# A decode block on one core: K in 64 KB packets with a two-part softmax, wo in one load, and the last transpose through a bf16 PSUM tile

## The chip, the cores and the metric

One core of a Trainium2 chip runs the whole program. The metric is the device time of one execution in microseconds (us); the kernel before takes 420.02 us, the median of three executions (419.86 to 420.03). "Landing" is the moment when a load's completion record of a DMA engine appears in the trace; a load has 16 of them, one from each engine, and I give the first and the last where they differ. "Lead" is how long before the landing (first engine) of the load ahead of it a load is issued: a positive lead means that the queue still has work when the next load arrives.

## The reference

Two batch rows with one token each, model width 1024, 32 query heads and 4 key-value heads of width 128, a cache of 32768 rows, and an MLP of width 3584. All inputs are bf16.

```python
    mod = (_silu(c) @ w_mod).reshape(c.shape[0], 6, 1, -1)
    sa, ca, ga, sb, cb, gb = ...                                  # six rows of mod
    h = _layernorm(x) * (1 + ca) + sa
    # attention: q = h @ wq; scores = q k^T * Dh ** -0.5; p = softmax(scores); (p v) @ wo
    x = x + ga * _A_ref(h, A_k_cache, A_v_cache, A_wq, A_wo)
    h = _layernorm(x) * (1 + cb) + sb
    # MLP: y = layernorm(h); gelu(y @ w1 + b1) @ w2 + b2
    x = x + gb * _B_ref(h, B_w1, B_b1, B_w2, B_b2)
```

There are 8 pairs of batch row and key-value head. Each pair has a K and a V of 32768 x 128 bf16, which is 8.4 MB each: 64 KB on each of 128 partitions. They are the bulk of the 178 MB that the kernel reads.

## The kernel before

One queue, issued from SyncE, brings everything in a fixed order into a ring of 160 KB per partition: w_mod, wq, then K and V of 8 rounds, then wo, w1, w2. A load is issued when the readers of the memory that it overwrites are done. K uses bytes 0 to 64 KB in two halves, V uses 64 to 128 KB.

```python
    def add_k(i, hf):
        add(("K", i, hf), [2, TPC * D], A_k_cache[i % 2, i // 2].rearrange("(p h c t) d -> h p c (t d)", h=2, c=2, p=128)[hf], hf * 32 * KB, f"K{hf}")

    def add_v(i):
        add(("V", i), [NCH, TPC * D], A_v_cache[i % 2, i // 2].rearrange("(p c t) d -> p c (t d)", c=NCH, p=128), 64 * KB, "V")
    # ...
    for i in range(NBG):
        add_k(i, 0)
        add_k(i, 1)
        add_v(i)
    for m, off in enumerate((128, 0)):
        add(("wo", m), [16, DM], A_wo[m * 2048:(m + 1) * 2048, :].rearrange("(p j) n -> p j n", j=16), off * KB)
```

A round works through four chunks of 8192 cache rows. PE turns K in groups of eight 128x128 tiles into PSUM (`tr`), VectorE (DVE) or ScalarE (ACT) evacuates each group, and PE multiplies it with the query (`qk`). Only after the last chunk come one maximum, the exponentials of all chunks, and then the product with V (`pv`).

```python
EVAC_PATTERN = ("dve", "act", "dve", "act", "dve", "dve", "act", "dve")
# ...
        for cc in range(NCH):
            for g8 in range(TPC // 8):
                tr(i, cc, g8)
                pipe.append((i, cc, g8))
                # ...
                if len(pipe) > PIPE:
                    qk(*pipe.pop(0))
        while pipe:
            qk(*pipe.pop(0))
        softmax_1()
        softmax_2()
        softmax_3()
        for cc in range(NCH):
            exp(cc)
        for cc in range(NCH):
            part_sum(cc)
            pv(i, cc)
        row_sums()
        extract()
        extract_2(i)
```

The last lines of the program turn the result so that it can be stored, through an fp32 PSUM tile:

```python
    pe(lambda e: e.matmul(psM[0:16, 0:128], lhsT=res_bf.rearrange("p b k -> p (b k)"), rhs=ident[:, :], start=True, stop=True),
       reads=["res_bf", "ident"], writes=["psM"])
    dve(lambda e: e.tensor_copy(res16[:, :], psM[0:16, 0:128]), reads=["psM"], writes=["res16", "c16"])
```

## Time and profile before

| | before |
|---|---|
| time, median of 3 | 420.02 us (419.86 to 420.03) |
| span of the profiled run | 418.7 us |
| busy: PE, DVE, ACT | 291.0, 209.6, 149.4 us |
| DMA queue's share of 16 engines | 98.8% |
| read | 178.28 MB, 426 GB/s over the span |
| round of the loop, V landing to V landing | 38.68 us |

The profile's page, the table of busy time by stretch and the chain are read in the prediction. This is the time line of SyncE of the kernel before (start, duration, engine, line, operation, out<-in, count):

```profile
102.47 0.33 SPq L389 DMA_DIRECT2D V<-in_A_v_cache_dram  x1
137.97 0.33 SPq L389 DMA_DIRECT2D V<-in_A_v_cache_dram  x1
174.92 0.33 SPq L389 DMA_DIRECT2D V<-in_A_v_cache_dram  x1
```

These three V are free to start when the K ahead of them has landed, which the completion records show at 108.90, 147.59 and 186.28 us (first engine). The leads are 6.4, 9.6 and 11.4 us. The queue is never near running dry.

### The profile page before, as it was taken

The numbers are of one execution on the slowest core, as the hardware profiler recorded it, in microseconds if no ns is written. First come the engines' busy times: TensorE is split into PE (matmuls) and PEld (weight loads), VectorE is DVE, ScalarE is ACT, GpSimd is POOL, SyncE is SP. The second block draws the span as 40 slices with busy tenths as digits, with TensorE's granted clock in tenths as the row PEclk, the third lists the DMA queues.
The fourth block names the chain that finished last, engine by engine and source line by source line (L and its number), as shares of the span: only waits on it lengthen the run. The fifth ranks groups of instructions, "written<-read, shape, count | busy, mean of one in ns | idle before, by whom it ended". The sixth has DMA issues, their size and how long they took to land.

```text
span 418.7 us, 11609 instructions
## 1 busy us (share of the span) xinstructions
PE 291.0 (70%) x5183; PEld 231.3 (55%) x5183; DVE 209.6 (50%) x423; ACT 149.4 (36%) x179; POOL 6.8 (2%) x29
## 2 busy tenths in 40 slices
PE   1407449766996895699369957976995699564536
PEld 1104219762993794299149926962894399221214
DVE  1201105546677676467726664766477567620411
ACT  2000015533565364256405632643365166400100
POOL 3000000000000000000000000000000000000000
PEclk9999557986896997799589958986697889576585
DMA  9989999999999999999999999999999999899995
GB/s 373 450 380 449 448 404 493 398 406 446 441 432 429 423 451 429 419 454 457 391 435 476 407 416 448 438 438 426 438 438 426 416 460 457 377 448 428 424 427 249
DMA packets 5581, 178.42 MB, mean 426 GB/s; under 512 B 698, under 2 KB 706, under 8 KB 964
## 3 DMA queue, kind: packets, MB, share of 16 engines
q1 hardware_dynamic: 5572, 178.28, 98.8%
q8 instruction: 8, 0.13, 0.1%
q14 instruction: 1, 0.01, 0.0%
HBM read 178.28 MB, written 0.00 MB: 426 GB/s over the span
## 4 chain that ended last, share of the span: by engine, by line
DMA 71%; PE 24%; DVE 2%; issue 1%; ACT 1%; SPq 1%
DMA V<-in_A_v_cache_dram 39%; DMA wo<-in_A_wo_dram 10%; DMA K<-in_A_k_cache_dram 10%; PE psZ L584 10%; DMA w<-in_B_w_dram 9%; PE psKT L536 8%; DMA wmod<-in_w_mod_dram 4%; PE psS L548 1%; PE psZ L548 1%; PE psS L655 1%; PE psZ L729 1%; PE psZ L469 1%; ACT KT_sb L540 0%; PE psS L469 0%; DVE m1c L553 0%
## 5 line engine op out<-in xcount | busy, mean ns | idle before, releaser
L536 PE MATMUL psKT<-ident,K 128*128 128x128 bf16 x2048 | 163.1, 229 | 11.5 <-DMA K<-in_A_k_cache_dram 11.5
L540 ACT ACTIVATE KT_sb<-psKT 128x1024 bf16<-128x1024 bf16 x96 | 98.2, 1025 | 124.4 <-PE psKT L536 124.4
L542 DVE COPY KT_sb<-psKT 128x1024 bf16<-128x1024 bf16 x160 | 106.7, 688 | 61.6 <-PE psKT L536 61.2
L536 PEld LDWEIGHTS psKT<-ident,K 128*128 128x128 bf16 x2048 | 126.7, 102 | 13.0 <-DMA K<-in_A_k_cache_dram 12.7
L584 PE MATMUL psZ<-V,E_sb 128*32 128x512 bf16 x512 | 46.4, 541 | 23.2 <-DMA V<-in_A_v_cache_dram 20.0
L548 PE MATMUL psS<-qcur,KT_sb 128*128 128x8 bf16 x1024 | 44.7, 167 | 2.2 <-issue 2.2
L584 PEld LDWEIGHTS psZ<-V,E_sb 128*32 128x32 bf16 x512 | 18.7, 130 | 47.7 <-issue 38.8
L548 PE MATMUL psZ<-qcur,KT_sb 128*128 128x8 bf16 x1024 | 43.0, 167 | 2.2 <-issue 1.5
L548 PEld LDWEIGHTS psS<-qcur,KT_sb 128*128 128x128 bf16 x1024 | 40.0, 97 | 2.3 <-issue 2.3
L548 PEld LDWEIGHTS psZ<-qcur,KT_sb 128*128 128x128 bf16 x1024 | 37.9, 96 | 3.4 <-issue 1.6
L572 ACT ACTIVATE E_sb<-S_sb 128x512 bf16<-128x512 f32 x32 | 19.5, 630 | 29.6 <-DVE S_sb L570 29.6
L570 DVE TENSOR_TENSOR S_sb<-S_sb,gmb 128x512 f32<-128x512 f32 x32 | 20.0, 685 | 0.3
L576 DVE TENSOR_REDUCE rs<-E_sb 128x8 f32<-128x512 bf16 x32 | 19.7, 675 | 0.0
L469 PE MATMUL psS<-wmod,inT 128*32 128x512 bf16 x32 | 5.1, 624 | 16.2 <-DMA wmod<-in_w_mod_dram 16.2
L553 DVE TENSOR_REDUCE m1c<-psZ 128x8 f32<-128x512 f32 x16 | 11.1, 693 | 10.2 <-ACT S_sb L552 10.1
L595 DVE RECIPROCAL rinv<-psM 128x1 f32<-128x1 f32 x8 | 1.3, 168 | 27.7 <-PE psM L593 27.7
L605 PE MATMUL psM<-msum,hmat 128*128 128x128 f32 x16 | 4.2, 347 | 13.3 <-DVE msum L600 13.3
L559 PE MATMUL psM<-identf,m 128*8 128x128 f32 x16 | 4.3, 369 | 13.1 <-DVE m L556 13.1
L553 DVE TENSOR_REDUCE m1c<-psS 128x8 f32<-128x512 f32 x16 | 11.1, 693 | 3.2 <-ACT S_sb L552 3.1
L552 ACT ACTIVATE S_sb<-psZ 128x512 f32<-128x512 f32 x16 | 9.5, 595 | 7.5 <-PE psZ L548 7.5
L477 DVE COPY S_sb<-psS 128x512 f32<-128x512 f32 x1 | 0.7, 690 | 22.9 <-PE psS L469 22.9
L469 PEld LDWEIGHTS psS<-wmod,inT 128*32 128x32 bf16 x32 | 1.1, 132 | 19.3 <-DMA wmod<-in_w_mod_dram 18.0
(123 smaller groups left out, 167.5 us busy)
## 6 DMA issues: line engine op xcount, KB each, us to landing
K<-in_A_k_cache_dram SPq DMA_DIRECT2D x16, 4096.0 KB, 27.1
wq<-in_A_wq_dram SPq DMA_DIRECT2D x2, 4096.0 KB, 44.8
wo<-in_A_wo_dram SPq DMA_DIRECT2D x2, 4096.0 KB, 39.0
w<-in_B_w_dram SPq DMA_DIRECT2D x2, 3584.0 KB, 32.5
wmod<-in_w_mod_dram SPq DMA_DIRECT2D x1, 6144.0 KB, 29.8
w<-in_B_w_dram SPq DMA_DIRECT2D x3, 2048.0 KB, 37.8
wmod<-in_w_mod_dram SPq DMA_DIRECT2D x1, 4608.0 KB, 15.8
wmod<-in_w_mod_dram SPq DMA_DIRECT2D x1, 1536.0 KB, 6.0
```

What stands on the lines that cost most here:

```text
L469: pe(lambda e, w=it.view, k=k, kk=kk, ch=ch, n=n, q=q: e.matmul(bank[n][32 * q:32 * q + 32, :], lhsT=inT[:, k, :], rhs=w[:, kk, ch * 512:( ...
L536: pe(lambda e, kq=kq, jj=jj, w=kt, t=t: e.transpose(psKT[kq][:, jj * 128:(jj + 1) * 128], w[:, t, :], ident[:, :]), reads=[it.reg, "ident" ...
L540: act(lambda e, src=src: e.activation(KT_sb[g8][:, :, :], src, ACT.Copy), reads=[f"psKT{kq}"], writes=[f"KT_sb{g8}"], sem=f"ev{cc}_{g8}")
L542: dve(lambda e, src=src: e.tensor_copy(KT_sb[g8][:, :, :], src), reads=[f"psKT{kq}"], writes=[f"KT_sb{g8}"], sem=f"ev{cc}_{g8}")
L548: pe(lambda e, t=t, jj=jj: e.matmul(ps[:, t * HPG:(t + 1) * HPG], lhsT=KT_sb[g8][:, jj, :], rhs=qcur[:, :], start=True, stop=True), reads= ...
L552: act(lambda e: e.activation(Sc, ps.rearrange("p (t h) -> p h t", h=HPG), ACT.Copy), reads=[preg], writes=[f"S_sb_{cc}"], sem=f"sc{cc}")
L553: dve(lambda e: e.tensor_reduce(m1c[:, :, cc], ps.rearrange("p (t h) -> p h t", h=HPG), AX.X, ALU.max), reads=[preg], writes=[f"m1c{cc}"])
L559: pe(lambda e: e.matmul(psM[0:HPG, 0:128], lhsT=m1[:, :], rhs=identf[:, :], start=True, stop=True), reads=["m1", "identf"], writes=["psM"])
L570: dve(lambda e: e.tensor_tensor(Sc, Sc, gmb[:, :].unsqueeze(2).to_broadcast([128, HPG, TPC]), ALU.subtract), reads=[f"S_sb_{cc}", "gmb"], ...
L572: act(lambda e: e.activation(Ec, Sc.rearrange("p h (u t) -> p u h t", t=4), ACT.Exp, scale=SCALE), reads=[f"S_sb_{cc}"], writes=[f"E_sb_{c ...
L576: dve(lambda e: e.tensor_reduce(rs4[:, :, cc], Ec.rearrange("p u h t -> p h u t"), AX.XY, ALU.add), reads=[f"E_sb_{cc}"], writes=[f"rs4_{c ...
L584: pe(lambda e, t4=t4, tg=tg, q=q: e.matmul(psO[32 * q:32 * q + 32, :], lhsT=E_sb[:, tg // 4, :, :].rearrange("p h t -> p (h t)"), rhs=vt[: ...
```

## The change

The intent is to load K in one transfer with 64 KB to a partition, and wo as well, so that the same bytes go in half the packets. A whole K lands later than half a K, and it occupies one slot until all of it has been read. Two things pay for that. VectorE copies chunks 2 and 3 of K to a 32 KB side buffer, so that the slot comes free after two chunks. The softmax works in two parts, so that the product with V starts right behind the scores: chunks 0 to 2 with their own maximum, chunk 3 with its own, and weights bring the two together. The evacuation alternates evenly between VectorE and ScalarE, and the last transpose goes through a bf16 PSUM tile. The core of the diff:

```diff
+KC_AT = 128 * 1024
-W2_ITEMS = ((0, 8, 96), (8, 16, 112), (16, 24, 128), (24, 27, 144), (27, 28, 150))
-EVAC_PATTERN = ("dve", "act", "dve", "act", "dve", "dve", "act", "dve")
+W2_ITEMS = ((0, 8, 96), (8, 16, 112), (16, 24, 0), (24, 27, 16), (27, 28, 22))
+KEEP = {(0, 1): 0, (0, 3): 1, (0, 5): 2, (1, 1): 3}
 ...
-    def add_k(i, hf):
-        add(("K", i, hf), [2, TPC * D], ...[hf], hf * 32 * KB, f"K{hf}")
+    def add_k(i):
+        rows = A_k_cache[i % 2, i // 2].rearrange("(p c t) d -> p c (t d)", c=NCH, p=128)
+        if i:
+            add(("K", i), [NCH, TPC * D], rows, 0, "K", view=kv)
+            by_key["K2", i] = by_key["K", i]
+        else:
+            add(("K", i), [2, TPC * D], rows[:, 0:2, :], 0, sem="K", view=kv[:, 0:2, :])
+            add(("K2", i), [2, TPC * D], rows[:, 2:4, :], 32 * KB, sem="K2", view=kv[:, 2:4, :])
 ...
-    for m, off in enumerate((128, 0)):
-        add(("wo", m), [16, DM], ..., off * KB)
+    add(("wo", 0), [32, DM], A_wo.rearrange("(p j) n -> p j n", j=32), 0)
 ...
-        if EVAC_PATTERN[g8] == "act":
+        if g8 % 2:
 ...
+    def keep(i, n):
+        it = need("K2", i)
+        lo = n % 2 * 32 * D
+        dve(lambda e: e.tensor_copy(kc[:, n // 2, lo:lo + 32 * D], kv[:, 2 + n // 2, lo:lo + 32 * D]), reads=[it.reg], writes=[f"kc{n}"], sem=f"kc{n}")
 ...
                 tr(i, cc, g8)
+                if (cc, g8) in KEEP:
+                    keep(i, KEEP[cc, g8])
 ...
+                if (cc, g8) == (3, 2):
+                    max_1()
+                if (cc, g8) == (3, 4):
+                    max_2(0)
+                if (cc, g8) == (3, 6):
+                    max_3(0)
+        exp(0)
+        exp(1)
         while pipe:
             qk(*pipe.pop(0))
-        softmax_1()
-        softmax_2()
-        softmax_3()
-        for cc in range(NCH):
-            exp(cc)
-        for cc in range(NCH):
-            part_sum(cc)
-            pv(i, cc)
-        row_sums()
-        extract()
+        exp(2)
+        pv(i, 0)
+        max_2(1)
+        part_sum(0)
+        pv(i, 1)
+        max_3(1)
+        exp(3)
+        weights()
+        pv(i, 2)
+        part_sum(1)
+        part_sum(2)
+        weights_2()
+        extract(0)
+        pv(i, 3)
+        part_sum(3)
+        row_sums()
+        row_sums_2()
+        extract(1)
         extract_2(i)
 ...
-    pe(lambda e: e.matmul(psM[0:16, 0:128], lhsT=res_bf..., rhs=ident[:, :], start=True, stop=True), ...)
-    dve(lambda e: e.tensor_copy(res16[:, :], psM[0:16, 0:128]), ...)
+    pe(lambda e: e.transpose(psKT[0][0:16, 0:128], res_bf.rearrange("p b k -> p (b k)"), ident[:, :]), ...)
+    dve(lambda e: e.tensor_copy(res16[:, :], psKT[0][0:16, 0:128]), ...)
```

The places not shown set up the weights, the side buffer, other places in the ring for w1, the reordered extraction of the attention result into one tile `atT` for all heads, and the single loop over wo.

## The prediction

> **What bounds the kernel now.** I read the page's slices and queue table first, then the table of busy time by stretch, then the chain that ended last, then the order of time around single rounds and the tail. The page:
>
> ```profile
> PE   1407449766996895699369957976995699564536
> DMA  9989999999999999999999999999999999899995
> DMA packets 5581, 178.42 MB, mean 426 GB/s; under 512 B 698, under 2 KB 706, under 8 KB 964
> q1 hardware_dynamic: 5572, 178.28, 98.8%
> ```
>
> PE has holes in every round; the DMA row has none from the first slice to the last. So no engine's work is the bound; the bytes are. By stretch, cut at the landings of V (columns: length, then PE, PEld, DVE, ACT, POOL busy, clock, DMA share, GB/s):
>
> ```profile
> 130.00:168.70 38.70, 28.86 (x586) 24.52 (x586) 28.11 (x54) 20.35 (x26) 0.44 (x2) 0.85 1.00 434
> 284.70:323.40 38.70, 31.20 (x584) 26.96 (x584) 23.54 (x45) 17.07 (x21) 0.44 (x2) 0.81 1.00 434
> 411.00:418.70 7.70, 5.03 (x105) 4.59 (x105) 0.73 (x4) 0.00 (x0) 0.00 (x0) 0.50 0.44 179
> ```
>
> A round of the loop (one K and one V, 16.8 MB) takes 38.7 us whatever the engines do, at DMA share 1.00 and 434 GB/s. PE is busy 29 to 31 us of it. Only the last 7.7 us leave the DMA partly idle. In the chain, "V waits" are queueing: V is issued 32 us before it lands because other transfers stand ahead of it. The chain's end and one round in order of time:
>
> ```profile
> 174.92 32.74 DMA V<-in_A_v_cache_dram
> 207.66 0.14 issue
> 207.79 5.20 PE psZ L584 x49
> 213.04 33.25 DMA V<-in_A_v_cache_dram
> ...
> 413.27 1.87 PE psZ L729 x64
> 415.17 1.03 PE psZ L729 x32
> 416.22 0.19 DVE mT L732
> 416.43 0.24 DVE res_bf L733
> 416.72 0.29 PE psM L734
> 417.03 0.28 DVE c L736
> ```
>
> The end is: last w2 bytes land (the last completion records are at 415.4 us), 8 to 32 small matmuls, two vector operations, one transposing matmul, one copy, the store. I also take from the trace's packet records, each a transfer to one partition: a 32,768-byte packet takes 1213 ns, a 65,536-byte one 2418 ns. From its completion records: a V lands 19.32 us after the K half ahead of it (149.30 to 168.62), two K halves take 19.36 us (168.62 to 187.98). The same two numbers recur in every round.
>
> **What the Trainium skill says.** (1) "DMA: Bandwidth & Descriptors", section Bandwidth, "Where 436 GB/s comes from": 16 ports of 32 bytes at 850 MHz give 435.2 GB/s as the ceiling. The loop's measured 434 GB/s agrees; there is 0.3% above it. (2) "VectorE: DVE Perf Modes", section "The perf-mode tier table": a bf16 SBUF-to-SBUF copy may run at four elements a cycle, one from PSUM at two at most. The trace has only the second: 1024 bf16 from PSUM in 688 ns, which is 1024/2/0.96 = 533 ns plus 155. No run here shows the first yet. (3) "TensorE: Matmul & The Clock Gate", Part 1: an idle window of about 3.4 us halves the PE clock and a busy one restores it. The trace agrees: granted clock 0.5 to 67.65 us, though PE had started at 62.45; eight transposes took 0.87 us before and 0.47 us after.
>
> **The change part by part.**
>
> K packets. Rounds 1 to 7 load K in one transfer, 64 KB to a partition, instead of two of 32 KB. Each of 16 DMA engines had 16 packets of 1213 ns = 19.408 us a round and now has 8 of 2418 = 19.344, so 0.064 us less; the completion records say 19.36 against 19.32, so 0.04 less. Times 7 rounds: 0.28 to 0.45 us. Round 0 keeps two halves. All of this lies on the bounding resource.
>
> wo. Two halves become one load: another 0.04 to 0.06 us by the same working. It also moves the first half of the output projection later. Before, 32 matmuls ran at 372.1 and 32 at 381.73 to 385.3. Now all 64 start near 381. At the cold 3.3 to 3.5 us per 32 that is 6.8 us, at half warm about 5.5, so the residual, the two layernorms and w1 start 1.5 to 3.3 us later. In this tail gT was ready at 402.74 and the first w2 matmuls at 403.68 waited for their data anyway; the next wait for w2 is 4.2 us (to 408.41). A delay of up to 3.3 us is swallowed there. No cost.
>
> The copy ("keep") of half of K. K now fills one 64 KB slot, which would be free only after all transposes; so the kernel copies chunks 2 and 3 to a 32 KB side buffer, four copies of 128x4096 bf16 per round on DVE. Estimate, with the skill's four a cycle and the 155 ns above: 4096/4/0.96 + 155 = 1.22 us, 4.9 us a round. DVE gives up 4 evacuations of 0.688 (2.8 us), ACT gains 4 of 1.025 (4.1 us). A few small vector operations (weights, a second maximum, four more accumulations at 0.35 us) add about 3.5 us. DVE goes from about 24 us busy a round to about 30, ACT from 17 to about 21: both under 38.7.
>
> Two-part softmax. Maximum and exponentials of chunks 0 to 2 begin before the last scores, so PV starts right behind QK instead of after the gap seen here (L548 ended near 161.6, exponentials ready at 168.4). It adds one maximum pass (two fp32 matmuls of 0.4 to 0.6 us and 0.7 us of DVE). It pays for K landing whole: before, half a K was there 9.7 us earlier.
>
> The last transpose. fp32 to bf16 cast of 128 columns from PSUM, 0.28 us, becomes bf16 to bf16; at two a cycle 67 of 133 ns go: about 0.07 us less, on the path. The matmul stays 128 columns.
>
> Sum: 0.28 to 0.45 (K), 0.04 to 0.06 (wo), eight fewer completion packets of 9 ns (0.07), 0.07 (tail): 0.4 to 0.65 us less, unless a transfer has to wait for its buffer. I take 0.42: 419.6 us.
>
> **Whether a buffer stalls the DMA** (steady round, K landed at 0, V lands at 19.3, next K at 38.7). The next K needs the first 16 groups transposed and four copies done. Before, the same 16 groups freed K at 188.40 from a start at 178.65: 9.8 us. Add 2.5 us for a cold clock and 1.5 for DVE being over full at three copies in six groups: 14 us, needed at about 17.8 (19.3 less 1.5 for issue). Slack 4 us. The next V needs PV done: QK took 21.3 us (178.65 to 199.9), plus 3 to 4 as before, plus PV with the second maximum inside, 6 to 7.5: 31 to 33 us, needed at about 37. Slack 4 us or more. Round 0 is tighter: the copies wait in DVE's order for the second K half (landed 71.9 us), so QK is held from about 66 to 74; it then pays the two halts of 1.49 and 2.24 us named "issue" that this first pass shows. K free near 84.5, needed at 88; V free near 105, needed at 107.5. That the two evacuating engines have room for the moved work shows in their groups, where the idle time ahead of them is as large as the work, and ended by PE:
>
> ```profile
> L540 ACT ACTIVATE KT_sb<-psKT 128x1024 bf16<-128x1024 bf16 x96 | 98.2, 1025 | 124.4 <-PE psKT L536 124.4
> L542 DVE COPY KT_sb<-psKT 128x1024 bf16<-128x1024 bf16 x160 | 106.7, 688 | 61.6 <-PE psKT L536 61.2
> ```
>
> **Rivals.** A: the copies run at one element a cycle (4096/0.96 = 4.3 us, 17 us in the first part of a round with 4 us of other DVE work). Then K is free at 22 us or later and each of 7 rounds halts the DMA for 4 us or more: 445 to 450 us. For it: the one copy of 128x1024 that the trace has at one a cycle took 1054 ns (a broadcast source, though). Against: source and destination are contiguous bf16 in SBUF. 3%. At two a cycle (2.3 us) the slack of 4 us still holds. B: round 0 or the first rounds are late once, by 1 to 2 us, as PE starts 8 us later and cold. Then the DMA row gets one dent and the time is 420.5 to 421.5. For it: slack of only about 2 us in my sum, and instruction halts that I cannot place exactly. 17%. C: the intended gain is larger, some per cent, because the wait of PV or of QK was on the path. Against: DMA share 1.00 in every round. Even at 435.2 GB/s throughout, 178.28 MB take 409.7 us, and with some 2 us of start and the 4 us tail 415 or so: 1.2% is the most that anything can bring without fewer bytes. 1% for over 2%.
>
> **Range and chances.** The centre is 419.6; the spread of the three runs before is 0.17 us. Low end 419.1, if the full packet sum counts and the tail gives a little more; high end 420.9, with one late buffer. Faster by over 2% would need under 411.6: 0.01. Slower by over 2% needs over 428.4, rival A or a stall in each round: 0.04. Same: 0.95.
>
> **What would show each step.** Right: 65,536-byte packets for K, DMA share 1.00 and 434 GB/s in each round, rounds shorter by about 0.04 us, K issued 3 us or more before V ends, and the copies near 1.2 us each. PE's time would lie in one block per round with one wait, for K, in place of two. The last copy would be near 0.21 us. Wrong: a slice of DMA under 9 inside the loop, a K or V issue later than the landing of the transfer before it, copies over 3 us, or a w2 matmul that waits for gT after its data have landed.

## The result

| | before | after |
|---|---|---|
| time, median of 6 (range) | 420.01 us (419.86 to 420.07) | 419.76 us (419.61 to 421.40) |
| packets | 5581 | 4429 |

The six runs of the changed kernel are 421.40, 419.80, 419.61, 420.25, 419.64 and 419.73 us. The ratio of times, after over before, is 1.0002 with a 95% interval of 0.9987 to 1.0017: the same. (A ratio is the mean time of one kernel's runs over the mean of the other's of the same rounds, so it is not quite the ratio of the medians quoted.) So the median fell by 0.25 us while the mean did not fall at all, because two of the six runs are late by 0.5 and 1.7 us. The kernel before has none like the second of these: in all 46 of its runs told here the highest is 420.55 us. The profile happened to be taken in the run of 421.40 us, so the page below is of a late run. A second trace of the same kernel comes with the experiments.

The page of the changed kernel, the lines that answer to those in the prediction:

```profile
PE   1407434989499588939975995789398749956465
DMA  9989999999999999999999999999999999999994
DMA packets 4429, 178.42 MB, mean 425 GB/s; under 512 B 570, under 2 KB 578, under 8 KB 836
q1 hardware_dynamic: 4420, 178.28, 98.4%
```

There are 1152 packets fewer, the bytes are the same, and the DMA row still has no dent in the loop. What differs is the last slice, a 4 for a 5: a late end. By stretch, cut at the landings of V (length, then PE, PEld, DVE, ACT, POOL busy with counts, clock, DMA share, GB/s):

```profile
91.05:130.20 39.15, 30.79 (x544) 25.96 (x545) 28.11 (x58) 19.55 (x25) 0.51 (x2) 0.83 1.01 431
130.20:168.85 38.65, 31.05 (x621) 27.26 (x618) 28.98 (x60) 22.95 (x28) 0.51 (x2) 0.91 1.00 434
```

A round in the steady part is 38.65 us at share 1.00 and 434 GB/s. VectorE is busy 29.0 us of it, before 23.5 to 28.1 in the stretches that the prediction shows, and ScalarE 23.0 (before 17.1 to 20.4). The first stretch is 0.5 us longer than the second. The groups of the evacuation and of the new copy:

```profile
L570 DVE COPY kc<-kv 128x4096 bf16<-128x4096 bf16 x32 | 38.9, 1216 | 7.9 <-DMA kv<-in_A_k_cache_dram 7.9
L563 ACT ACTIVATE KT_sb<-psKT 128x1024 bf16<-128x1024 bf16 x128 | 128.4, 1024 | 99.5 <-PE psKT L559 99.5
L565 DVE COPY KT_sb<-psKT 128x1024 bf16<-128x1024 bf16 x128 | 88.0, 689 | 61.4 <-PE psKT L559 61.0
```

The copy takes 1216 ns; the prediction had 1.22 us from the four elements a cycle of the skill's table. Both engines still stand idle for long before their evacuations (99.5 and 61.4 us in sum), and PE ends that idle time. So neither engine became the bound.

The room is smaller than the busy times suggest, though. PE works through a round in order, waiting for DVE and ACT on the way, and where it waits for a load there is room. Two such waits of a round before (in brackets, us), and the one that is left in the changed kernel:

```profile
169.11 5.76 PE L584 MATMUL psZ<-V,E_sb 128*32 128x512 bf16 x64 [4.10 <-DMA V<-in_A_v_cache_dram]
178.65 1.96 PE L536 MATMUL psKT<-ident,K 128*128 128x128 bf16 x32 [1.31 <-DMA K<-in_A_k_cache_dram]
```

```profile
188.56 3.56 PE L559 MATMUL psKT<-ident,kv 128*128 128x128 bf16 x32 [1.27 <-DMA kv<-in_A_k_cache_dram]
```

From the third round on, PE waits for K between 0.1 and 1.6 us a round, in this trace and in the second one. From the start of a round's scores to PE's last matmul for it the chain of PE and the engines that it waits for takes 37.1 to 38.1 us of the 38.64. keep_twice below shows what happens when it takes longer.

SyncE's time line of the changed kernel shows how the leads have shrunk:

```profile
83.28 0.33 SPq L410 DMA_DIRECT2D kv<-in_A_k_cache_dram  x1
106.56 0.33 SPq L410 DMA_DIRECT2D V<-in_A_v_cache_dram  x1
125.13 0.33 SPq L410 DMA_DIRECT2D kv<-in_A_k_cache_dram  x1
143.76 0.33 SPq L410 DMA_DIRECT2D V<-in_A_v_cache_dram  x1
```

The loads ahead landed at 89.39, 108.73, 128.47 and 147.79 us (first engine), so the leads are 6.1, 2.2, 3.3 and 4.0 us. In the later rounds they lie between 4.0 and 5.6 us. The prediction counted its slack from 1.5 us before the landing. Its slack of 4 us or more in steady rounds is therefore a lead of about 5.5 us or more, and its 2.5 us (107.5 less 105) for the first V a lead of about 4. The measured leads, 4.0 to 5.6 us and 2.2 us (4.7 in the second trace), are somewhat smaller. Before, V had 6 to 12 us.

The tail of the changed kernel, from the time line:

```profile
382.51 5.59 PE L723 MATMUL psS<-wo,atT 128*32 128x512 bf16 x64 [1.32 <-POOL atT L667]
...
406.50 1.47 PE L788 MATMUL psS<-w,gT 128*32 128x512 bf16 x16 [2.27 <-DVE gT L779]
408.96 1.90 PE L788 MATMUL psS<-w,gT 128*32 128x512 bf16 x16 [0.99 <-DMA w<-in_B_w_dram]
...
418.48 0.21 DVE L803 COPY c<-psKT 16x128 bf16<-16x128 bf16 x1 [0.37 <-PE psKT L802]
```

The output projection starts at 382.51 us, and what it waited for in this late trace is the attention result (POOL at L667), not wo; in the second trace it waited for wo and started at 381.36 us. The first w2 matmuls wait for gT, 3.7 us later than before (406.45 against 402.74), but the next ones wait for data again. In the second trace gT comes at 406.84 us, 4.1 us later than before, and only one wait for data is left after it, of 0.34 us at 412.93. So the delay is swallowed, with little to spare. The last copy takes 0.21 us; before it took 0.28.

### The profile page after: what moved, and what is told of

Its sections match the earlier page's. It is cut to its first block, busy times and chain, and to the rows that moved or that the text cites. A ratio compares the mean times of both kernels' runs of the same rounds, so it can differ in the third digit from the quotient of the medians.

```text
span 420.1 us, 11896 instructions
## 1 busy us (share of the span) xinstructions
PE 292.4 (70%) x5215; PEld 238.3 (57%) x5215; DVE 246.5 (59%) x535; ACT 181.9 (43%) x219; POOL 7.3 (2%) x28
## 2 busy tenths in 40 slices
DMA packets 4429, 178.42 MB, mean 425 GB/s; under 512 B 570, under 2 KB 578, under 8 KB 836
## 4 chain that ended last, share of the span: by engine, by line
DMA 59%; PE 22%; DVE 10%; issue 5%; ACT 3%; SPq 0%; ACTq 0%; DVEq 0%; POOL 0%
DMA kv<-in_A_k_cache_dram 45%; PE psKT L559 13%; DMA wmod<-in_w_mod_dram 7%; DMA w<-in_B_w_dram 6%; ACT KT_sb L563 3%; DVE KT_sb L565 2%; DVE kc L570 2%; PE psS L576 2%; DVE m1c L580 2%; PE psZ L576 1%; PE psZ L628 1%; PE psS L723 1%; DVE msum L651 1%; PE psZ L797 1%; PE psZ L490 1%
## 5 line engine op out<-in xcount | busy, mean ns | idle before, releaser
L563 ACT ACTIVATE KT_sb<-psKT 128x1024 bf16<-128x1024 bf16 x128 | 128.4, 1024 | 99.5 <-PE psKT L559 99.5
L565 DVE COPY KT_sb<-psKT 128x1024 bf16<-128x1024 bf16 x128 | 88.0, 689 | 61.4 <-PE psKT L559 61.0
L559 PE MATMUL psKT<-ident,kv 128*128 128x128 bf16 x1024 | 91.6, 250 | 10.9 <-DMA kv<-in_A_k_cache_dram 10.8
L559 PEld LDWEIGHTS psKT<-ident,kv 128*128 128x128 bf16 x1024 | 74.2, 114 | 12.8 <-DMA kv<-in_A_k_cache_dram 12.8
L559 PE MATMUL psKT<-ident,kc 128*128 128x128 bf16 x1024 | 78.9, 220 | 0.0
L559 PEld LDWEIGHTS psKT<-ident,kc 128*128 128x128 bf16 x1024 | 58.9, 98 | 2.1 <-issue 2.0
L576 PEld LDWEIGHTS psZ<-qcur,KT_sb 128*128 128x128 bf16 x1024 | 37.1, 96 | 12.2 <-ACT KT_sb L563 12.2
L570 DVE COPY kc<-kv 128x4096 bf16<-128x4096 bf16 x32 | 38.9, 1216 | 7.9 <-DMA kv<-in_A_k_cache_dram 7.9
L628 PE MATMUL psZ<-V,E_sb 128*32 128x512 bf16 x384 | 27.0, 401 | 1.3 <-ACT E_sb L602 1.3
L581 ACT ACTIVATE S_sb<-psS 128x512 f32<-128x512 f32 x16 | 9.6, 597 | 20.4 <-DVE m1c L580 20.4
L628 PEld LDWEIGHTS psZ<-V,E_sb 128*32 128x32 bf16 x384 | 10.7, 99 | 8.2 <-ACT E_sb L602 2.0
## 6 DMA issues: line engine op xcount, KB each, us to landing
w<-in_B_w_dram SPq DMA_DIRECT2D x1, 768.0 KB, 28.1
```

The source lines that it names most:

```text
L559: pe(lambda e, kq=kq, jj=jj, w=kt, t=t: e.transpose(psKT[kq][:, jj * 128:(jj + 1) * 128], w[:, t, :], ident[:, :]), reads=[k_reg, "ident"] ...
L563: act(lambda e, src=src: e.activation(KT_sb[g8][:, :, :], src, ACT.Copy), reads=[f"psKT{kq}"], writes=[f"KT_sb{g8}"], sem=f"ev{cc}_{g8}")
L565: dve(lambda e, src=src: e.tensor_copy(KT_sb[g8][:, :, :], src), reads=[f"psKT{kq}"], writes=[f"KT_sb{g8}"], sem=f"ev{cc}_{g8}")
L570: dve(lambda e: e.tensor_copy(kc[:, n // 2, lo:lo + 32 * D], kv[:, 2 + n // 2, lo:lo + 32 * D]), reads=[it.reg], writes=[f"kc{n}"], sem=f" ...
L576: pe(lambda e, t=t, jj=jj: e.matmul(ps[:, t * HPG:(t + 1) * HPG], lhsT=KT_sb[g8][:, jj, :], rhs=qcur[:, :], start=True, stop=True), reads= ...
L581: act(lambda e: e.activation(Sc, ps.rearrange("p (t h) -> p h t", h=HPG), ACT.Copy), reads=[preg], writes=[f"S_sb_{cc}"], sem=f"sc{cc}")
```

## The experiments

All are edits of the changed kernel. The theory: the loop and the tail gain what the packets and the last copy say, about 0.4 us, in every undisturbed run; some runs lose it again, because a load now comes too late for the running queue or because one DMA engine falls behind. The rivals: that the gain in the loop doesn't exist (rival C of the prediction turned round: fewer packets do nothing), that the tail or the new work on VectorE takes it back, or that the late runs are noise that both kernels have. Times are medians with the range; "before" is of the same rounds, and on the same chip. By the record's limit of 2%, keep_twice is slower, late_v_msum unclear, and all others are the same; so differences of a few tenths rest on the landings in the traces and not on the times.

| run | time, us | before, us | range, us |
|---|---|---|---|
| after_again | 419.73 (419.57 to 421.43) | 420.12 | 1.86 |
| k_halves | 420.02 (419.95 to 421.58) | 420.08 | 1.63 |
| v_quarters | 420.64 (420.57 to 420.79) | 420.08 | 0.22 |
| v_halves | 419.99 (419.92 to 420.08) | 420.12 | 0.16 |
| tail_undone | 419.94 (419.66 to 420.49) | 420.08 | 0.83 |
| keep_later | 420.16 (419.59 to 421.39) | 420.08 | 1.80 |
| evac_mix | 420.26 (419.86 to 421.76) | 420.12 | 1.90 |
| v1_halves | 420.20 (419.75 to 421.34) | 420.07 | 1.59 |
| one_softmax | 425.82 (422.90 to 427.21) | 420.07 | 4.31 |
| late_v_rsum | 424.48 (423.74 to 425.24) | 420.07 | 1.50 |
| late_v_msum | 429.56 (427.73 to 430.52) | 420.07 | 2.79 |
| keep_twice | 452.88 (451.36 to 454.45) | 420.07 | 3.09 |

### after_again: the changed kernel once more

No edit.

> The changed kernel itself, for its spread on this chip beside the two below. Theory (its loads are issued 2 to 5 us before the queue runs dry, and those under 3 us leave single DMA engines behind, which shows as a late straggler at the end): median near 419.8, but single runs up to 421.4, a range of over 1 us where the kernel before has 0.2. Rival (the one run of 421.4 was chance of the chip): all runs within 419.6 to 420.0.

Six more runs: 419.57, 421.43, 419.62, 420.15, 419.85 and 419.57 us. The spread is real and belongs to the kernel: of its 12 runs eight lie between 419.57 and 419.85 (mean 419.67), two at 420.15 and 420.25, two at 421.4. The trace of this label is of a run of 419.57 us, which makes two traces of one kernel, a late one and a good one. The landings of three traces (us, first engine unless noted; the last column from the time line):

| trace | V of round 1 | V of round 7 | wo | last byte, last engine | store issued |
|---|---|---|---|---|---|
| before | 128.23 | 360.32 | 379.70 | 415.43 | 417.34 |
| after_again (419.57) | 128.18 | 360.02 | 379.34 | 415.05 | 416.89 |
| after (421.40) | 128.47 | 360.30 | 379.66 | 416.81 | 418.72 |

Take the differences row by row. Before to after_again, the store comes 0.45 us earlier: 0.05 up to the first V of the table, 0.25 in the six rounds between the V (232.09 against 231.84 us), 0.06 in wo (19.38 against 19.32), 0.02 in w1 and w2, and 0.07 after the last byte (1.91 against 1.84). These are the prediction's terms for K, wo and the tail. The late trace gains the same 0.26 us in its rounds (231.83). Against after_again it loses 0.29 ahead of them, 0.04 in wo, 1.44 in w1 and w2 (37.15 against 35.71) and 0.07 after the last byte, less the 0.01 of its rounds; that is the 1.83 us between the two stores. The end of the work after the last byte, time line of the late trace and then of the good one:

```profile
414.84 2.80 PE L797 MATMUL psZ<-gT,w 128*128 128x2 bf16 x96 [1.31 <-DMA w<-in_B_w_dram]
```

```profile
412.93 2.88 PE L797 MATMUL psZ<-gT,w 128*128 128x2 bf16 x96 [0.34 <-DMA w<-in_B_w_dram]
```

Both wait for data; in the late trace PE waits 1.0 us longer and starts 1.9 us later.

*The first loss.* In the late trace V of round 1 was issued at 106.56 us with 2.2 us of lead, in the good one at 104.19 with 4.7. The engines then paused 0.52 us on average before the first byte of that V, against 0.00. Why was it issued late? The stretch from 92 to 98 us, in which PE works through the first round's scores, late trace first:

```profile
92.00:98.00 6.00, 5.98 (x99) 5.50 (x100) 3.56 (x9) 2.54 (x3) 0.00 (x0) 0.72 1.00 429
```

```profile
92.00:98.00 6.00, 5.34 (x124) 4.90 (x122) 4.54 (x10) 3.68 (x5) 0.00 (x0) 1.00 1.02 440
```

The granted clock was 0.72 against 1.00, and 99 matmuls were done in the time of 124. Just ahead of this stretch PE had stood still for 1.60 us in the late trace and for 1.05 in the good one (both put down to "issue"; a 16 KB transfer of the instruction queue starts just ahead of each, at 89.67 and 89.59 us). A longer halt came before the slower clock, but two traces don't prove that the one causes the other. The page of the Trainium skill that the prediction names ("TensorE: Matmul & The Clock Gate", Part 1) doesn't settle it: it speaks of an idle window of about 3.4 us, about twice this halt.

*The second loss.* In the late trace two of the 16 engines end late: one brings its last byte at 415.90 us, one at 416.81, the other 14 by 415.25. The packet records show a 16 KB transfer of the queue that the page lists as "q8 instruction" at 387.9 us, during w1, and another at 410.5 us, during w2. At the first, one engine goes from 0.78 to 2.20 us behind the first engine to land; at the second, another goes from 1.69 to 3.12, and this is the one that ends last. In the trace of before the same two fetches, at 386.1 and 407.1 us, move engines from 0.08 to 1.49 and from 0.05 to 1.47 us; in the good trace, at 386.9 and 410.4 us, from 0.10 to 1.55 and from 0.12 to 1.54. So a fetch goes with a loss of about 1.4 us for one engine in all three, and what differs is which engine that is: one from the front ends level with the slowest, one from further back ends last, alone. Three milder late traces below end in the same way: the last fetch sets an engine from 0.62 to 2.04 us behind (keep_later), from 1.05 to 2.47 (v1_halves) and from 0.91 to 2.30 (tail_undone). In the late trace the pause before V of round 1 had changed the order in which the engines land; in the good one the order stayed. This reading is worked out from records in time order; no run takes the fetch away, so it stays an inference.

### k_halves: K in halves again, all else as changed

```diff
-        if i:
-            add(("K", i), [NCH, TPC * D], rows, 0, "K", view=kv)
-            by_key["K2", i] = by_key["K", i]
-        else:
-            ...                     # the two halves, now in every round
+        add(("K", i), [2, TPC * D], rows[:, 0:2, :], 0, sem="K", view=kv[:, 0:2, :])
+        add(("K2", i), [2, TPC * D], rows[:, 2:4, :], 32 * KB, sem="K2", view=kv[:, 2:4, :])
```

> The changed kernel with K again in two 32 KB loads in every round; nothing else undone. Theory (the DMA sets the time; larger packets save only what the packet records say): a round's period between V landings goes from 38.64 back to 38.68 us, so the time rises by 0.3 us, to about 420.05; too small for the timed runs, clear in the landings. Rival A (K landing whole delays QK and that costs time): as fast or faster than the changed kernel, 419.3 or less. Rival B (packet size is worth more than the records say): 420.5 or more.

Five of six runs lie between 419.95 and 420.11 us, one at 421.58. The six rounds between the V landings take 232.09 us (128.15 to 360.24), exactly what the kernel before takes and 0.26 more than the changed kernel. The gain of the loop is the gain of the K packets, and it disappears with them. The late run shows that the spread doesn't come from the 64 KB packets of K; V and wo still have them.

### v_quarters: the packet cost made larger

```diff
     def add_v(i):
-        add(("V", i), [NCH, TPC * D], ..., 64 * KB, "V")
+        rows = A_v_cache[i % 2, i // 2].rearrange("(p c t) d -> p c (t d)", c=NCH, p=128)
+        for c in range(NCH):
+            add(("V", i, c), [TPC * D], rows[:, c, :], (64 + 16 * c) * KB, f"V{c}")
```

> The changed kernel with V in four loads of 16 KB to a partition, the packet effect made larger. Theory: a 16 KB packet takes 611 ns where a quarter of a 64 KB one is 604.5; 32 a round on each engine are 0.21 us, three more completion records 0.03; times 8 rounds 1.9 us by the packet sum, about 1.2 if it shrinks between landings as it did for K (0.04 for 0.064): 420.9 to 421.7. Rival B (a fixed cost for each issue beside the packets, some 0.1 us or more on an idle queue between loads): 24 more loads make 422.2 or more. Rival C (packet size does nothing): 419.8.

420.64 us, 1.0 us above the good runs of the changed kernel (419.67), and a little less than expected. A 16,384-byte packet takes 611 ns, so four make 2444 against 2418 for one of 64 KB: 26 ns times 8 packets times 8 rounds is 1.7 us. The landings say less and are right: the V of round 1 takes 19.45 us (109.10 to 128.55), though 32 packets of 611 ns on an engine sum to 19.55; the six rounds take 232.61 us, which is 38.77 a round against 38.64; 0.13 times 8 is 1.0. So smaller packets do make the loop longer, and the durations of single packets overstate by how much.

One rival stands: a fixed cost for each load, smaller than rival B's. Every load of weights or cache has 8 packets on each engine, so half the packet size means twice the loads as well, and no run changes the one without the other. The landings fit a line in the load's size: about 0.044 us a load and 0.3012 us for each KB of a partition (19.32 us at 64 KB, 9.68 at 32, 8.48 at 28, 4.86 at 16). K in one load saves one such 0.044 us, V in quarters adds three. For the change the two come to the same. The page counts

```profile
DMA packets 7886, 178.43 MB, mean 426 GB/s; under 512 B 954, under 2 KB 962, under 8 KB 1220
```

The range is only 0.22 us. That was not what I was looking for, and it was the first sign of where the spread comes from: with V in pieces, its first piece is issued as soon as the first chunk of the old V has been read.

### v_halves: V in two loads

```diff
-        add(("V", i), [NCH, TPC * D], ..., 64 * KB, "V")
+        for h in range(2):
+            add(("V", i, h), [2, TPC * D], rows[:, 2 * h:2 * h + 2, :], (64 + 32 * h) * KB, f"V{h}")
```

> The changed kernel with V in two loads of 32 KB to a partition, so that the first is issued when two chunks of PV are done, some 4 us earlier. It gives up in packets what K gained (8 times 0.04 us). Theory: no load has a lead under 3 us, so the runs lie close together (range under 0.4 us), at 419.8 to 420.1. Rival (the spread has another cause): a range of over 1 us as in the changed kernel.

419.99 us with a range of 0.16, as tight as the kernel before. SyncE's time line (the count x2 means both halves; the second is issued 3.0 us after the first):

```profile
99.42 3.32 SPq L412 DMA_DIRECT2D V<-in_A_v_cache_dram  x2
139.96 3.32 SPq L412 DMA_DIRECT2D V<-in_A_v_cache_dram  x2
```

The leads are 9.4 us and 7.5 us, where the changed kernel has 2.2 to 4.7 and 4.0 to 5.5. The loop pays the packets back (232.08 us for six rounds), so nothing is gained over before except wo and the tail. The spread goes when V has plenty of lead, as far as five runs of this kernel and five of v_quarters can show it.

### tail_undone: wo in halves and the fp32 transpose

```diff
-    add(("wo", 0), [32, DM], A_wo.rearrange("(p j) n -> p j n", j=32), 0)
+    for m in range(2):
+        add(("wo", m), [16, DM], ...[:, 16 * m:16 * m + 16, :], 32 * m * KB)
 ...
-    pe(lambda e: e.transpose(psKT[0][0:16, 0:128], ...
+    pe(lambda e: e.matmul(psM[0:16, 0:128], ...
```

> The changed kernel with wo in two loads of 32 KB to a partition and the result turned through an fp32 PSUM tile. Theory: wo takes 0.04 us more, the last copy 0.28 instead of 0.21 us, so 0.1 us more, 419.9; the first wo matmuls still start near 382.5, since they wait for the last round's attention result and not for wo. Rival (the early half of wo matters): gT comes 3 us earlier and the time falls below 419.5.

419.94 us, best run 419.66; the profiled run is a late one (420.47). The first wo matmuls start at 381.32 us, after the attention result, and gT is ready at about 404.5, 2 us earlier than in the traces of the changed kernel. The rival put the time below 419.5 then; it isn't. wo takes 19.38 us from the V ahead of it (360.09 to 379.47), as before, against 19.32 in after_again, and the last copy 0.28 against 0.21. The two parts are there in the trace at their predicted sizes, 0.06 and 0.07 us; the times of whole runs, spread over 0.83 us, neither show nor deny them.

### keep_later: the copies two groups later

```diff
-KEEP = {(0, 1): 0, (0, 3): 1, (0, 5): 2, (1, 1): 3}
+KEEP = {(0, 3): 0, (0, 5): 1, (0, 7): 2, (1, 1): 3}
```

> The changed kernel with three of the four copies of K two groups later, so that in round 0 DVE blocks on the second K half two groups later. Theory (V of round 1 is issued at 106.56 us, only 2.2 us before the K ahead of it ends, and this lost 0.4 us of DMA once): that V is issued about 1 to 2 us earlier, the gap before its landing shrinks below 0.1 us, the time is 419.3 to 419.4. Rival (the 0.4 us have nothing to do with the issue): V lands at 130.2 as before and the time stays at 419.8.

A miss. The first part went as intended: V of round 1 is issued at 103.50 us with 5.4 us of lead, without a pause. But the times are 419.59 to 421.39, with the spread that I wanted to take away. The price is on the other load: K's leads fell to between 3.0 and 4.0 us in the later rounds. The pauses behind them are small (0.04 us at most in the mean), but one engine ended at 415.56 us, after the fetch at 410.4, with the others by 415.07. So a good lead of the first V alone doesn't remove the spread.

### evac_mix: more evacuations on VectorE

```diff
-        if g8 % 2:
+        if g8 in ((1, 3, 5, 7) if cc == 0 else (1, 3, 6)):
```

> The changed kernel with the evacuations of chunks 1 to 3 shared as before (five on DVE, three on ACT, where the copies no longer load DVE), packets untouched. Theory: ACT no longer holds QK up (0.3 to 0.8 us a chunk), V is issued 1 to 1.5 us earlier in each round, leads 5 us or more except in round 0 with 3 to 4; fewer starved engines: 419.3 to 419.6 with a range under 0.8 us, the best of all. Rival: the time does not move with the lead, 419.8 with the same spread as the changed kernel.

A miss as well. ACT's work fell from 22 to 19 us a round and DVE's rose from 29 to 30.5, but the scores were not done sooner: V of round 2 was issued at 142.34 us, against 143.76 and 141.96 in the two traces of the changed kernel. So moving evacuations from ScalarE to VectorE does not speed up the scores. The profiled run (419.86 us) has no pause; two of the timed runs are at 421.7.

### v1_halves: only the V of round 1 in halves

```diff
+        if i == 1:
+            add(("VX", i), [2, TPC * D], rows[:, 0:2, :], 64 * KB, sem="VX", view=vv[:, 0:2, :])
+            add(("V", i), [2, TPC * D], rows[:, 2:4, :], 96 * KB, sem="V", view=vv[:, 2:4, :])
+        else:
             add(("V", i), [NCH, TPC * D], rows, 64 * KB, sem="V", view=vv)
```

> The changed kernel with one load of it split: the V of round 1 comes in two loads of 32 KB to a partition, the first issued when two chunks of round 0's PV are done, some 5 us earlier; all other packets stay at 64 KB. Theory (the only load whose lead can fall under 3 us is that V, behind the first pass through the loop; a pause there leaves the DMA engines out of step, and the spread at the end comes from it): all runs at 419.5 to 419.8, range under 0.4 us, about 0.45 us under the kernel before, faster than both. Rival (the spread comes from elsewhere in the changed kernel): median 419.7 again with single runs at 421 or more.

This run didn't do what it was made for. The V of round 0 is one region in the kernel's bookkeeping, so both halves waited for its last reader and were issued together:

```profile
106.03 0.80 SPq L416 DMA_DIRECT2D vv<-in_A_v_cache_dram  x2
```

The lead was 2.9 us, not 9. So the theory behind it was not tested. The run reproduces the late case instead: packets of up to 1980 ns (1213 is usual) as this V starts, an engine that goes from 0.65 to 2.06 us behind at w1 and ends at 415.55, and another that the fetch at 410.2 us sets back and that brings the last byte at 415.96; the times reach 421.34.

### one_softmax: the softmax of before in the changed kernel

```diff
-        exp(0)
-        exp(1)
         while pipe:
             qk(*pipe.pop(0))
-        exp(2)
-        pv(i, 0)
-        ...                                # the two parts
+        softmax_1()
+        softmax_2()
+        softmax_3()
+        for cc in range(NCH):
+            exp(cc)
+        for cc in range(NCH):
+            part_sum(cc)
+            pv(i, cc)
```

> The changed kernel with the softmax of before: one maximum over all four chunks, then all exponentials, then PV. K in 64 KB packets, wo in one load and the last transpose stay. Theory (K landing whole leaves the V buffer free only some 5 us before the queue runs dry; the two-part softmax is what pays for it): V is issued about 5 us later in each round, the lead falls to about 0, the DMA pauses 1 to 2 us in each round and more in round 0: 428 to 434 us, DMA share below 0.98 in each round. Rival (PE has room anyway, since it is idle 8 us a round): 419.8, DMA share 1.00.

425.82 us, ratio 1.0147 (1.0117 to 1.0178) to before: slower, clear of the noise though under 2%, and by 5.8 us rather than 8 or more. In its trace, which is of the fastest of the four runs (422.90 us), the leads of V fell to between 0.4 and 3.1 us, and its pauses are 0 to 1.2 us. So the two-part softmax is not an ornament: without it K in one load loses more than ten times what its packets gain. It was milder than expected because a paused V gives the next one lead back, as the next run shows.

### late_v_rsum and late_v_msum: V issued later on purpose

The issue of V also waits for a vector result of the round: for the row sums, or for the end of the accumulation (msum).

```diff
-            T.dma("sp", lambda e, dst=dst, src=cur.src: e.dma_start(dst, src), key=cur.sem, writes=[cur.reg], frees=old)
+            T.dma("sp", lambda e, dst=dst, src=cur.src: e.dma_start(dst, src), key=cur.sem, writes=[cur.reg], frees=old,
+                  after=["rsum16"] if cur.key[0] == "V" and cur.key[1] else [])
```

> The changed kernel with one wait more: V of the next round is issued only when this round's row sums are spread, about 3.2 us after its buffer is free; compute is untouched. Theory (a load issued less than about 3 us before the load ahead of it ends leaves some DMA engines dry): lead 2.0 us instead of 5.2, a pause of about 0.5 us in rounds 1 to 6 and 3 us in round 0: about 425. Rival (a load only has to be issued before the one ahead ends): only round 0 loses, about 1 us: 420.8.

> As the one before, but V waits for the end of the accumulation, about 5.2 us after its buffer is free, so that the lead is 0. Theory: a pause of about 1.5 us in rounds 1 to 6 (half of the 3 us needed, as each pause moves the next K too and gives the other half back) and some 5 us in round 0: 432 to 435. Rival: no pause in rounds 1 to 6 and 3 us in round 0: 423.

424.48 and 429.56 us (ratios 1.0107 and 1.0218). The first is what was expected in sum, though its leads are not 2.0 us in each round but vary from -0.4 to 3.1. With msum the V of rounds 1 to 4 are issued so:

```profile
110.84 0.33 SPq L410 DMA_DIRECT2D V<-in_A_v_cache_dram  x1
...
149.31 0.33 SPq L410 DMA_DIRECT2D V<-in_A_v_cache_dram  x1
...
191.17 0.33 SPq L410 DMA_DIRECT2D V<-in_A_v_cache_dram  x1
...
228.19 0.33 SPq L410 DMA_DIRECT2D V<-in_A_v_cache_dram  x1
```

Their leads are -1.9, 1.8, -1.4 and 3.2 us, their mean pauses 3.1, 0.0, 3.0 and 0.0. They alternate: when V pauses, the next K lands later, while the next V's release doesn't move, so it has the lead back. Every second round pays, which is why the time is less than my sum over all rounds (432 to 435).

From these runs and the rest, pause against lead, the mean of the 16 engines:

| lead, us | mean pause, us | runs |
|---|---|---|
| -2.4 to -1.6 | 3.1 to 4.0 | keep_twice |
| -1.9, -1.4 | 3.1, 3.0 | late_v_msum |
| -0.4 | 1.7 | late_v_rsum |
| 0.25 to 0.8 | 0.6 to 1.2 | keep_twice, one_softmax |
| 1.1 to 1.9 | 0.0 to 0.8 | late_v_msum, late_v_rsum, keep_twice, one_softmax |
| 2.0, 2.2 | 0.44, 0.52 | late_v_rsum, after |
| 2.2 to 2.5 | 0.0 to 0.15 | late_v_rsum, keep_twice, one_softmax |
| 2.8 to 3.2 | 0.0 to 0.13 | late_v_rsum, keep_later, one_softmax, tail_undone, v1_halves |
| 3.2 and more | mostly 0.00 to 0.05, twice 0.09 and 0.13 | all |

Two kinds of load are left out: the K of round 1 (0.2 to 0.3 us at leads of 6 to 7; two or three fetches that set one engine of 16 back by 1.4 us each come to as much) and the V of round 7, whose landing records mix with others. Up to about 1.6 us the pause is roughly 1.6 us less the lead. Between 1.6 and 3 us some engines still pause. Above that almost nothing is lost. The packet records of the driest queues (keep_twice, late_v_msum) show where the 1.6 us go: the first data packet starts 0.95 us after the issue, the last engine's 1.5 to 2.0 us after it, and these first packets take about 3.1 us instead of 2.42.

### keep_twice: each copy done twice

```diff
-        dve(lambda e: e.tensor_copy(kc[...], kv[...]), reads=[it.reg], writes=[f"kc{n}"], sem=f"kc{n}")
+        for s in ("kd", "kc"):
+            dve(lambda e: e.tensor_copy(kc[...], kv[...]), reads=[it.reg], writes=[f"kc{n}"], sem=f"{s}{n}")
```

> The changed kernel with each of the four copies of K done twice: 4.9 us more DVE work in the first third of a round. Theory: K is free 2.5 to 4 us later, so its lead falls from 4.8 us to about 1 to 2, and QK and with it V come later by as much: pauses of 0.5 to 1.5 us a round, 423 to 430. Rival (DVE has 10 us of idle time a round, so this is hidden): 419.8.

452.88 us, ratio 1.0793: much worse than expected. The stretch from 170 to 210 us of this kernel and one issue from its time line:

```profile
170.00:210.00 40.00, 31.37 (x557) 27.39 (x555) 30.18 (x60) 21.11 (x26) 0.50 (x2) 0.82 0.93 393
```

```profile
217.76 0.33 SPq L410 DMA_DIRECT2D kv<-in_A_k_cache_dram  x1
```

The DMA share is 0.93 and 393 GB/s. This K is issued 17.4 us after its round's scores began (200.33); in the changed kernel it is 12.35 (188.56 to 200.91). The 5 us between are the four extra copies of 1.2 us. Its lead is -2.4 us and its pause 4.0, and six of the seven K have leads of -1.6 to -2.4 us and pauses of 3.1 to 4.0. My expectation took the give-back of V for K too, and that was the error. The time line shows why nothing is given back. K had landed at 196.34 us (last engine), but the scores began only 4.0 us later, straight behind the extraction of the round before:

```profile
199.74 0.80 PE L657 MATMUL psM<-msum,hmat 128*128 128x128 f32 x2 [1.67 <-DVE msum L652]
...
200.33 3.62 PE L559 MATMUL psKT<-ident,kv 128*128 128x128 bf16 x32
```

From the second round on, K lands 2.9 to 4.2 us before its scores begin, and between 160 and 325 us PE doesn't wait for a load at all. So here the bound is no longer the queue but the engines' chain, with DVE's copies in it: from one start of the scores to the next it takes 42.8 us on average (156.91 to 371.02, five rounds). In the changed kernel PE waits 0.1 to 1.6 us a round for K; the 4.9 us of copies use this up and add the rest, about 4 us, to each round. The prediction's rival A rests on slow copies that make each round longer in this way. Its copies of 17 us, against 9.7 here, would by the same sum, which is an estimate, have cost more than its 445 to 450 us.

## Why the prediction was right

*The bound.* DMA share 1.00 and 434 GB/s in every steady round, before and after: right. PE, with its clock between 0.72 and 1.00 at different times, doesn't set the length of a steady round. The prediction's block of PE work with one wait a round, for K, is in the trace too; that this wait is only 0.1 to 1.6 us was not foreseen.

*K packets.* Predicted 0.28 to 0.45 us for seven rounds. Measured 0.25 us for six, which is 0.29 for seven: the low end, that of the completion records. The term worked out from packet durations (0.45) was too large by a half, as v_quarters shows again. k_halves takes the gain away and nothing else of the loop's length. The sum's extra 0.07 for completion records was counted twice beside the times from landing to landing, which contain these records. Whether the gain belongs to the packets or to the loads is open (v_quarters).

*wo and the last copy.* Predicted 0.04 to 0.06 and 0.07; measured 0.06 and 0.07 (0.28 to 0.21 us). The output projection was to start when wo has landed, near 381 us. It did in the good trace (381.36); in the late one it waited for the attention result until 382.51, since the last round's extraction now ends about 7 us after its product with V instead of 3.4. The delay at gT, 4.1 and 3.7 us, is above the 3.3 that I had, and it was swallowed all the same, in the good trace with 0.34 us left. (The 4.2 us that I read for the wait are those of the weight load; the matmuls at 408.41 waited 3.69.) I had named "a w2 matmul that waits for gT after its data have landed" as a sign of being wrong. It happened (406.50) and cost nothing, as the next wait, at 408.96, is for data again (in the good trace the one at 412.93). The sign should have been: the last wait before the end is for gT.

*The copies and the engines' room.* 1.22 us predicted, 1.216 measured; DVE about 30 us a round predicted, 29.0 measured; ACT about 21 predicted, 21 to 23 measured. But these sums of busy time say little about the room: DVE has 9 us of idle time a round, and the chain that it stands in has 0.1 to 1.6.

*Slack.* About 4 us in steady rounds, which with the 1.5 us for the issue is a lead of 5.5 or more: measured leads 4.0 to 5.6 from round 2 on. Round 0: K freed near 84.5 predicted, 83.28 measured; V near 105 predicted, 104.19 and 106.56 measured. The requirement was mis-sized: I took 1.5 us for the issue, and a lead up to about 3 us is needed for all engines to run on undisturbed. With 1.5 the first V's slack looked safe in most runs; with 3 it is on the edge.

*The rivals.* A is refuted by the 1216 ns; keep_twice shows that its cost was put too low. C is refuted by the ceiling: the share was and stays 1.00. B, one late buffer in round 0, was given 17%, and something like it happens in about a third of the runs: four of 12 are at 420.15 or above. In the one late trace it is rival B (0.3 to 0.5 us) and, which the prediction didn't have, a DMA engine that ends alone 1.4 us late.

*The number.* 419.6 is where the undisturbed runs are (mean of eight 419.67; best 419.57). The mean of all 12 is 420.05, level with before, because the late runs give back the gain. The range, 419.1 to 420.9, holds the time of before as well, so the median inside it is no proof of the mechanism; the landings are. That the median of six shows the gain at all is partly luck, as about a third of the runs are late and the mean shows none.

*What stays open.* Of the late runs only the one of 421.40 and the milder ones of keep_later, tail_undone and v1_halves (420.18 to 420.57) have a trace; the four agree on the last fetch, not on a pause of the first V. keep_later and evac_mix have a first V with 4.5 us of lead or more in their traces, and late runs among their timed ones. Only the two kernels whose V has 7 us of lead or more in the rounds looked at, v_halves and v_quarters, and the kernel before are steady. That short leads make the spread, by changing the order of the engines before a fetch, fits these runs; it is not shown. v1_halves was made to decide it and failed to.

No version here beats both kernels clearly. v_halves is the steadiest of the changed ones and 0.13 us below before of the same rounds; the changed kernel as it is has the best runs.

## What to carry to other kernels

When the DMA queue is full from end to end, count only what a change does to the bytes and packets, and to the few microseconds after the last byte; here all else in it, an engine's extra 5 us a round and a restructured softmax, served only to keep the queue full. Then list each load's lead before and after: a change that moves no median can still spend the lead, and below some 3 us it begins to cost in some runs and not in others. Measure also the engines' chain through a round, and not their busy times: none was busy for more than about 31 of 38.6 us, yet PE waited at most 1.6 us for K, and 4.9 us more of copies made each round about 4 us longer. A V issued late on purpose, with no engine work added, gave its loss back in the next round.

## What the Trainium skill lacked or had wrong

- "DMA: Bandwidth & Descriptors", section "Latency and other measured facts", gives about 600 ns to the first byte of a load on the hardware queues (HWDGE). On a queue that had run dry the traces have 0.95 us from SyncE's issue to the first data packet, and 1.5 to 2.0 us to that of the last of 16 engines. The page has no figure for how long before the end of the load ahead the next must be issued. The runs show a pause of roughly 1.6 us less the lead, and small pauses of single engines up to a lead of about 3 us (0.52 us on average at 2.2).
- No page that I found has what an instruction fetch does to the data queue: in the traces each 16 KB fetch of the tail goes with one engine falling about 1.4 us further behind (0.08 to 1.49, 0.78 to 2.20, 1.69 to 3.12). The cause is inferred from the times.
- On what the prediction took from the skill, the traces agree: 434 GB/s under its ceiling of 435.2, and four elements a cycle for a bf16 copy in SBUF (1216 ns for 4096 elements).
